# All exponent biases on VectorE in a fused attention and mixing kernel, with the order, bank and engine tables set anew

## The chip, the cores and the metric

The kernel runs on one core of one Trainium2 chip. The metric is the device time of one execution in microseconds. A core has TensorE (PE in the profile, with its weight loads as PEld), VectorE (DVE), ScalarE (ACT), GpSimd (POOL) and SyncE (SP), which here issues all DMAs. The engines run their own instruction lists in order and wait for each other by semaphores.

## What is computed

Attention over 8 batches of 8 heads with 576 positions of 64 channels, with a mask by blocks of 64 positions; then, for each batch, a mixing layer on the 576x512 result x:

```python
scores = scale * np.matmul(q, k.transpose(0, 1, 3, 2))
scores = np.where(block_i >= block_j, scores, -1000000000.0)
attn = np.exp(scores - np.max(scores, axis=-1, keepdims=True))
attn = attn / (np.sum(attn, axis=-1, keepdims=True) + 1e-09)
x = np.matmul(attn, v)                       # heads side by side: (B, 576, 512)
theta = x @ w_theta
y = w_tok_r @ (x * cos(theta)) + w_tok_i @ (x * sin(theta))
u = x + y
out = u + np.maximum(u @ w_ch, 0.0)
```

## The kernel before

**Parts.** The work is cut into some 3,400 parts, each of which issues one to some tens of instructions. Three tables of literals decide everything about them that is not fixed by the mathematics: `ORDER` is the sequence in which the parts are issued (each engine gets its instructions in this sequence), `BANKS` says which PSUM bank each result takes, and `PLACES` gives, for each part that has a choice, the engine: A is ScalarE, P is GpSimd, D is VectorE. `emit` reads the tables and calls the parts. Nothing is decided on the chip.

**A head of attention.** Heads come in pairs p, head n = 2p and 2p + 1. TensorE makes the scores (line 589, with the mask at 596 and the first block at 617) in PSUM (`s` and `g` are banks). VectorE takes the maxima of the four or five row tiles (`m`, line 633). The bias of the exponential, -scale times the maximum plus a constant, is one small instruction on `m` of 128 x 2 to 128 x 5 elements (line 641), part `mn`; ScalarE then makes the exponentials `t` (line 646), which wait for it. A copy in 16 bits `p` (the part `high`, line 431 on ScalarE, 433 elsewhere) and the rest of the difference (`low`, line 436) follow, SyncE issues a transposing DMA (`pt<-p`), and TensorE multiplies with v (`weighted`, line 680). VectorE divides by the sum (lines 692, 694 and 698) into `xn`. The first 16 heads have two pieces, A and B, with a bias each; the other 48 have one: 80 biases in all. The first three batches (24 heads) use a constant scale, the later ones a scale from the tile `size`.

**The mixing of a batch.** `xn` is split (`xp`, lines 431, 433 and 436), transposed by DMA (`xT`), and TensorE makes theta (816, 819). ScalarE and VectorE make the turns (828, 834), their absolute values (440 on ScalarE, 442 on VectorE) and the sines (849, 851). `z`, the product with x (line 860, GpSimd or VectorE), is split into `zh` and `zl`; TensorE mixes tokens (884), `u` is collected on VectorE (893, after `x_again`, line 889, on GpSimd or VectorE), split (423 or 427, and 900), and multiplied with the channel weights (907); the result goes out by 913 or 915 and 923. Once at the start, the weights are unpacked and split (lines 471 to 507).

The bias and its reader, and the line that adds the part with its choice of engines:

```python
        def bias(self, piece, on):                                          # line 638
            engine_of(on).tensor_scalar(out=self.m[:, NI + a:NI + b], in0=self.m[:, a:b],
                scalar1=self.scales()[1], scalar2=math.log(LIFT), op0=ALU.mult, op1=ALU.add)
...
            nc.scalar.activation(out=t_parts[self.hh][:, to:to + n], in_=self.scores_of(i), func=AF.Exp,
                scale=self.scales()[0], bias=self.m[:, NI + i:NI + i + 1])   # line 646
...
                add(("mn", n, piece), step_of(h.bias, piece), known + [("m", n, i) for i in mine], on="DP")
```

Of the kernel before, what the change touches and what calls it, by code (L numbers as in the profile page):

```python
# [37 lines left out]
    8, 160, 158, 16, 9, 10, 11, 17, 18, 335, 363, 339, 364, 372, 373, 374, 340, 0, 1, 350, 351, 19, 12, 352, 353,  # L38
    375, 336, 387, 2, 334, 361, 3, 362, 365, 24, 337, 386, 32, 33, 25, 56, 338, 341, 392, 376, 342, 26, 57, 40, 58,
    41, 366, 367, 20, 27, 162, 42, 4, 343, 368, 5, 48, 59, 49, 28, 391, 390, 354, 50, 43, 163, 13, 344, 21, 29, 34,  # L40
    385, 51, 35, 369, 415, 164, 401, 60, 165, 414, 388, 345, 72, 413, 44, 104, 64, 136, 88, 96, 80, 161, 346, 347,
    105, 106, 402, 403, 412, 166, 416, 167, 168, 389, 36, 65, 73, 89, 97, 423, 169, 52, 74, 170, 171, 172, 159, 90,
    393, 66, 394, 98, 332, 81, 355, 82, 137, 107, 75, 348, 437, 395, 67, 37, 396, 397, 398, 138, 120, 424, 333, 99,
    112, 383, 45, 53, 349, 404, 377, 76, 83, 384, 139, 100, 356, 61, 14, 91, 417, 84, 418, 68, 92, 69, 357, 441, 77,
    358, 85, 425, 359, 93, 101, 465, 370, 141, 151, 466, 121, 122, 436, 113, 176, 142, 143, 178, 144, 94, 371, 114,
    115, 439, 419, 360, 78, 378, 420, 489, 440, 116, 22, 399, 438, 443, 62, 123, 6, 38, 494, 379, 464, 421, 442,
    444, 380, 173, 452, 447, 445, 434, 540, 463, 467, 446, 145, 15, 128, 140, 426, 427, 174, 381, 468, 469, 70, 405,
    406, 474, 152, 453, 108, 448, 30, 487, 31, 435, 470, 449, 454, 86, 455, 456, 180, 400, 124, 129, 130, 471, 491,
    490, 495, 407, 514, 408, 409, 410, 488, 382, 475, 428, 476, 477, 478, 545, 496, 1804, 492, 422, 450, 497, 493,
# [12 lines left out]
    650, 673, 631, 604, 669, 611, 693, 1854, 1869, 651, 670, 646, 1855, 645, 656, 657, 1864, 639, 612, 613, 698,
    614, 1857, 1865, 652, 678, 658, 632, 564, 691, 1862, 196, 1858, 1859, 692, 633, 586, 615, 1863, 626, 653, 679,
    680, 681, 694, 695, 689, 659, 699, 700, 660, 682, 654, 661, 696, 701, 1908, 697, 1909, 744, 634, 1866, 721, 674,
    702, 1910, 720, 197, 1899, 729, 1914, 1915, 730, 707, 718, 635, 1870, 191, 1867, 1916, 1900, 1873, 1901, 199,
    636, 1871, 683, 690, 703, 719, 708, 709, 1885, 637, 675, 710, 722, 200, 676, 2004, 2007, 1881, 201, 119, 655,
    662, 663, 664, 665, 711, 1911, 749, 1884, 704, 1912, 705, 712, 1880, 2005, 155, 1907, 731, 1877, 1902, 723, 684,
    1893, 1917, 724, 202, 1903, 1894, 1895, 725, 1888, 1872, 1896, 1897, 1918, 1892, 666, 1898, 1913, 677, 203,
    1904, 2008, 1889, 2006, 1882, 685, 1919, 743, 1890, 1876, 1878, 1886, 1879, 742, 686, 1874, 1875, 1905, 687,
    726, 727, 785, 195, 732, 747, 748, 745, 746, 750, 753, 204, 706, 713, 205, 1944, 765, 714, 715, 716, 754, 751,  # L70
    752, 755, 733, 1945, 756, 764, 767, 766, 157, 1938, 1887, 1883, 1939, 734, 1940, 206, 768, 688, 771, 1946, 2009,
    790, 757, 1941, 758, 772, 769, 1891, 770, 773, 193, 1947, 207, 135, 208, 1937, 192, 1948, 1949, 1942, 1943, 717,
    2010, 735, 728, 736, 737, 738, 740, 739, 741, 783, 784, 786, 826, 2023, 788, 787, 789, 791, 2024, 759, 808,
# [24 lines left out]
    2123, 2124, 2125, 244, 2126, 968, 982, 2265, 969, 1041, 2143, 2150, 2127, 2151, 2128, 985, 970, 2135, 2257,
# [1078 lines left out]
```

## Time and profile before

| what | value |
|---|---|
| time, median of 3 runs (least to most) | 674.0 us (673.57 to 674.95) |
| time of the profiled execution | 677.03 us |
| its span, first to last instruction | 675.2 us |
| TensorE busy | 614.8 us, 91% |
| VectorE busy | 586.5 us, 87% |
| ScalarE busy | 508.3 us, 75% |
| GpSimd busy | 374.3 us, 55% |
| mean granted clock of TensorE | 0.964 |

The profiled execution is 3.0 us longer than the median, and its span is 1.8 us shorter than its own time. Busy shares are averages; the program has a start in which weights and inputs arrive, a long middle in which the heads of one batch run beside the mixing of the batch before, and an end that only mixes the last batch.

### The profile page before, as it was taken

How to read it: one execution, taken by the hardware profiler on the slowest of the kernel's cores; microseconds unless marked ns; L12 is line 12 of the kernel's file. 1: busy time of each engine (PE TensorE's matmuls, PEld its weight loads, DVE VectorE, ACT ScalarE, POOL GpSimd, SP SyncE). 2: the span in 40 equal slices, each digit the busy share in tenths (PEclk: the TensorE clock that was granted, in tenths of full speed). 3: DMA queues.
4: the chain of work that ended last, by engine and by line, in shares of the span. 5: the costliest groups of instructions: out<-in, count | busy, mean ns of one | idle time of the engine just before them, and what ended most of it. 6: DMA issues, size and time to landing. Idle time of an engine off the chain costs nothing.

```text
span 675.2 us, 18061 instructions
## 1 busy us (share of the span) xinstructions
PE 614.8 (91%) x7374; PEld 456.1 (68%) x7374; DVE 586.5 (87%) x1162; ACT 508.3 (75%) x770; POOL 374.3 (55%) x391
## 2 busy tenths in 40 slices
PE   5376688998999999999999998999899999999997
PEld 3155545785688577775787756785677477867775
DVE  3988889998997999989998899999998999976554
ACT  5888669885987998877998799979987997225021
POOL 2463536853667467961677628744593457931530
PEclk9577788999999999999999999999999999999999
DMA  8999999899969688879789977999779547930003
GB/s 349 336 264 224 196 196 225 183 202 187 202 141 237 132 190 188 183 157 185 202 178 154 206 168 169 199 165 213 169 177 184 93 81 161 189 78 2 19 1 123
DMA packets 268515, 116.58 MB, mean 173 GB/s; under 512 B 256016, under 2 KB 256016, under 8 KB 268432
## 3 DMA queue, kind: packets, MB, share of 16 engines
q1 hardware_dynamic: 268432, 115.43, 79.1%
q8 instruction: 57, 0.93, 0.6%
q14 instruction: 26, 0.21, 0.1%
HBM read 42.01 MB, written 9.44 MB: 76 GB/s over the span
## 4 chain that ended last, share of the span: by engine, by line
PE 52%; DVE 22%; DMA 10%; ACT 8%; POOL 4%; issue 4%; SPq 1%; ACTq 0%; POOLq 0%; DVEq 0%
PE g L884 12%; PE s L884 8%; DMA pt<-p 7%; PE g L680 7%; DVE m L633 5%; PE g L816 5%; PE g L907 5%; PE s L589 4%; PE s L907 4%; DVE p L436 3%; PE s L816 3%; ACT t L646 3%; PE g L589 2%; DMA xT<-xp 2%; PE s L819 1%
## 5 line engine op out<-in xcount | busy, mean ns | idle before, releaser
L884 PEld LDWEIGHTS <-zh 128*128 128x128 f16 x1152 | 112.7, 98 | 29.8 <-issue 1.1
L884 PE MATMUL g<-wT_h,zh 128*128 128x288 f16 x405 | 115.9, 286 | 1.0 <-DVE u L893 0.8
L884 PE MATMUL g<-wT_h,zl 128*128 128x288 f16 x405 | 115.8, 286 | 0.1
L884 PE MATMUL g<-wT_l,zh 128*128 128x288 f16 x405 | 115.8, 286 | 0.0
L680 PE MATMUL g<-v,pt 128*128 128x65 f16 x2880 | 102.9, 197 | 13.3 <-DMA pt<-p 6.5
L680 PEld LDWEIGHTS <-pt 128*128 128x128 f16 x2880 | 99.0, 100 | 20.3 <-DMA pt<-p 10.3
L633 DVE TENSOR_REDUCE m<-s 128x1 f32<-128x576 f32 (+2 forms) x132 | 85.3, 672 | 6.9 <-PE s L596 6.9
L436 POOL TENSOR_TENSOR p<-t,p 128x512 f16<-128x512 f32 (+4 forms) x28 | 66.5, 2376 | 43.8 <-ACT p L431 38.9
L431 ACT CAST p<-t 128x1600 f16<-128x1600 f32 (+4 forms) x66 | 84.3, 1283 | 8.5 <-DMA pt<-p 4.4
L436 DVE TENSOR_TENSOR p<-t,p 128x1600 f16<-128x1600 f32 (+4 forms) x52 | 84.9, 1635 | 5.0 <-ACT p L431 3.5
L860 POOL TENSOR_TENSOR aa<-aa,xn 128x256 f32<-128x256 f32 (+1 forms) x59 | 48.3, 832 | 60.3 <-ACT aa L849 44.4
L816 PEld LDWEIGHTS <-xT 128*128 128x128 f16 x384 | 36.6, 99 | 46.9 <-DMA xT<-xp 4.3
L884 PEld LDWEIGHTS <-zl 128*128 128x128 f16 x576 | 56.3, 98 | 16.3 <-issue 1.6
L646 ACT ACTIVATE t<-s,m,size 128x576 f32<-128x576 f32 (+1 forms) x80 | 59.1, 778 | 7.8 <-POOL m L641 6.5
L907 PEld LDWEIGHTS <-wch_h 128*128 128x128 f16 x512 | 48.1, 98 | 15.8 <-issue 2.8
L633 DVE TENSOR_REDUCE m<-g 128x1 f32<-128x192 f32 (+2 forms) x156 | 54.4, 372 | 4.5 <-PE g L596 4.4
L646 ACT ACTIVATE t<-g,m,size 128x320 f32<-128x320 f32 (+2 forms) x100 | 49.0, 535 | 11.9 <-DVE m L641 5.7
L436 POOL TENSOR_TENSOR zl<-aa,zh 128x512 f16<-128x512 f32 (+1 forms) x36 | 40.8, 1139 | 15.3 <-ACT zh L431 9.5
L884 PE MATMUL s<-wT_h,zh 128*128 128x288 f16 x171 | 48.9, 286 | 0.0
L884 PE MATMUL s<-wT_l,zh 128*128 128x288 f16 x171 | 48.9, 286 | 0.0
L884 PE MATMUL s<-wT_h,zl 128*128 128x288 f16 x171 | 48.9, 286 | 0.0
L907 PE MATMUL g<-uh,wch_h 128*128 128x288 f16 x160 | 45.8, 286 | 1.4 <-DVE u L893 0.8
(194 smaller groups left out, 1624.3 us busy)
## 6 DMA issues: line engine op xcount, KB each, us to landing
rv<-in_v SPq DMA_DIRECT2D x16, 768.0 KB, 5.4
rq<-in_q SPq DMA_DIRECT2D x16, 640.0 KB, 5.1
rk<-in_k SPq DMA_DIRECT2D x16, 576.0 KB, 5.0
out<-xT SPq DMA_DIRECT2D x32, 288.0 KB, 2.8
w_raw<-in_w_tok SPq DMA_DIRECT2D x5, 576.0 KB, 6.7
pt<-in_w_tok SPq DMA_DIRECT2D x4, 576.0 KB, 8.5
w_raw<-in_w_theta SPq DMA_DIRECT2D x4, 512.0 KB, 7.0
w_raw<-in_w_ch SPq DMA_DIRECT2D x4, 512.0 KB, 4.7
```

What stands on the lines that cost most here:

```text
L431: nc.scalar.copy(out=out, in_=x)
L436: engine_of(on).tensor_tensor(out=out, in0=x, in1=y, op=ALU.subtract)
L589: nc.tensor.matmul(to[hh][:, col:col + n], lhsT=qq[rows, P + P * i:P + P * i + P], rhs=kk[rows, k0:k0 + n], start=nn == 0 and col % 512 == ...
L633: nc.vector.tensor_reduce(out=self.m[:, i:i + 1], in_=self.scores_of(i), axis=AX.X, op=ALU.max)
L646: nc.scalar.activation(out=t_parts[self.hh][:, to:to + n], in_=self.scores_of(i), func=AF.Exp, scale=self.scales()[0], bias=self.m[:, NI + ...
L680: nc.tensor.matmul(o[:, i, :], lhsT=source[:, block, :], rhs=vv[:, slot, hh, :], start=first, stop=last)
L816: nc.tensor.matmul(g, lhsT=xT[:, xx + i, :], rhs=ww[:, dt, :], start=first, stop=last)
L819: nc.tensor.matmul(g[half * D:half * D + D, 0:HC], lhsT=xT[:, xx + i, 0:D], rhs=ww[:, dt, half * HC:half * HC + HC], start=first, stop=last)
L860: engine_of(on).tensor_tensor(out=cd, in0=cd, in1=self.xns[dt][:, i0:i0 + ni, :], op=ALU.mult)
L884: nc.tensor.matmul(g, lhsT=zz[:, kk, cols], rhs=ww[:, kk, ts], start=(n == 0 and kk == k0 and nn == 0), stop=n == 4 and kk == k0 + ni - 1 ...
L907: nc.tensor.matmul(g[:, 0:HS], lhsT=ww[:, dt, e * P:(e + 1) * P], rhs=uu[:, dt, th * HS:(th + 1) * HS], start=dt == 0 and n == 0, stop=dt ...
```

## The change

The code of the parts is the same. All three tables have other numbers, so that the order on every engine, the banks and the engines of other parts differ too. Of the 80 biases, 33 were on VectorE and 47 on GpSimd; now all 80 are on VectorE. The parts with a choice, before and after (A ScalarE, P GpSimd, D VectorE), as the tables give them:

| part | before | after |
|---|---|---|
| `mn`, bias | P 47, D 33 | D 80 |
| `high` | A 66, P 10, D 4 | A 65, P 8, D 7 |
| `low` | P 28, D 52 | P 23, D 57 |
| `z` | P 103, D 57 | P 111, D 49 |
| `zh` | A 43, P 26, D 11 | A 53, P 21, D 6 |
| `zl` | P 57, D 23 | P 58, D 22 |
| `x_again` | P 15, D 17 | P 19, D 13 |
| `xp`, both halves | A 21, P 26, D 17 | A 20, P 23, D 21 |
| absolute values of turns | A 28, D 12 | A 24, D 16 |
| first half of v | A 24, P 4, D 4 | A 16, P 13, D 3 |
| first half of u | A 20, P 8, D 4 | A 18, P 9, D 5 |
| first halves of q and k | A 25, P 11, D 4 | A 31, P 7, D 2 |
| unpacking and scaling of weights | A 24, P 12, D 15 | A 31, P 14, D 6 |

```diff
 ORDER = [
-    8, 160, 158, 16, 9, 10, 11, 17, 18, 335, 363, 339, 364, 372, 373, 374, 340, 0, 1, 350, 351, 19, 12, 352, 353,
...
 PLACES = (
-    "DAAPDAADPDDPAAAADDDADADAAAPDAPPDAPDPPAAPADAAPAAPADAADAPPADPPDPDPAPPPDAPPADDPDADADDPPDADPPPAPADDPDPAPPAPAPDDDAPPA"
...
+    "ADAAAAADPPAPAADPAAPAAPAAPAAADAADPAAAPAAADPPAPAAPAAPADDDDPDDPPDPDPDADDADDADDDDPDADDAPDAPDDPDDADDAPDAPDAPADADDAPDA"
```

**Heads 30 and 31 on VectorE**, some 280 us after the start, before the change (`p_99` and `p_100` are the `low` of an even and an odd head, here 30 and 29; the biases of both heads are on GpSimd here):

```order
L436 TENSOR_TENSOR p_100<-t_98,p_100 128x1536
L692 TENSOR_SCALAR r<-g_114 128x5
L633 TENSOR_REDUCE m<-s_110 128x1
L694 RECIPROCAL r<-r 128x5
L726 TENSOR_REDUCE size<-size 128x3
L633 TENSOR_REDUCE m<-g_112 128x1
L893 SCALAR_TENSOR_TENSOR u_3974<-g_111,size_tok,u_3974 128x288
L633 TENSOR_REDUCE m<-g_112 128x1
L382 TENSOR_REDUCE size<-g_111 128x3
L384 TENSOR_SCALAR size<-size 128x3
L387 TENSOR_SCALAR size<-size 128x3
L436 TENSOR_TENSOR p_99<-t_97,p_99 128x1600
```

The same place after the change:

```order
L633 TENSOR_REDUCE m<-s_110 128x1
L860 TENSOR_TENSOR aa<-aa,xn 128x2x128
L743 SCALAR_TENSOR_TENSOR size<-size,size_theta 128x1
L633 TENSOR_REDUCE m<-s_110 128x1
L641 TENSOR_SCALAR m<-m,size 128x4
L726 TENSOR_REDUCE size<-size 128x3
L893 SCALAR_TENSOR_TENSOR u_3943<-g_113,size_tok,u_3943 128x288
L692 TENSOR_SCALAR r<-g_114 128x5
L694 RECIPROCAL r<-r 128x5
L698 TENSOR_TENSOR xn<-g_114,r 128x5x64
L382 TENSOR_REDUCE size<-g_111 128x3
L436 TENSOR_TENSOR p_99<-t_97,p_99 128x1600
```

The bias of head 31 now stands on VectorE right behind the last of its maxima and ahead of the `low` of head 30 (`p_99`).

**The last two heads on VectorE** (62 and 63), some 574 us after the start, before:

```order
L923 SCALAR_TENSOR_TENSOR xT<-u_8605,size,s_109 128x288
L436 TENSOR_TENSOR p_99<-t_97,p_99 128x1600
L915 TENSOR_SCALAR g_113<-g_113,size 128x288
L923 SCALAR_TENSOR_TENSOR xT<-u_8110,size,g_113 128x288
L573 SCALAR_TENSOR_TENSOR v_88<-rv,size,v_87 128x12x64
L692 TENSOR_SCALAR r<-g_114 128x5
L694 RECIPROCAL r<-r 128x5
L698 TENSOR_TENSOR xn<-g_114,r 128x5x64
L860 TENSOR_TENSOR aa<-aa,xn 128x128
L915 TENSOR_SCALAR g_111<-g_111,size 128x288
L889 TENSOR_TENSOR u_9364<-xT 128x576
L692 TENSOR_SCALAR r<-g_114 128x5
```

After:

```order
L573 SCALAR_TENSOR_TENSOR v_86<-rv,size,v_85 128x12x64
L923 SCALAR_TENSOR_TENSOR xT<-u_8106,size,g_111 128x288
L860 TENSOR_TENSOR aa<-aa,xn 128x128
L436 TENSOR_TENSOR p_99<-t_97,p_99 128x1600
L436 TENSOR_TENSOR zl<-aa,zh 128x512
L692 TENSOR_SCALAR r<-g_114 128x5
L860 TENSOR_TENSOR rr<-rr,xn 128x2x128
L694 RECIPROCAL r<-r 128x5
L698 TENSOR_TENSOR xn<-g_114,r 128x5x64
L436 TENSOR_TENSOR p_100<-t_98,p_100 128x1536
L436 TENSOR_TENSOR zl<-rr,zh 128x512
```

Before, only head 62 has its `low` on VectorE (the row `p_99`), followed by an `x_again` (L889); now head 63 has its `low` there too (`p_100`), and the `x_again` is elsewhere.

**VectorE at the start**, some 20 to 30 us after it, among the unpacking of weights (L481, L485, L501) and the first maxima, before:

```order
L481 TENSOR_SCALAR w_raw<-w_raw 128x576
L485 SCALAR_TENSOR_TENSOR w_val<-w_val,pt_107 128x576
L485 SCALAR_TENSOR_TENSOR w_val<-w_val,w_raw 128x576
L485 SCALAR_TENSOR_TENSOR w_val<-w_val,pt_106 128x576
L436 TENSOR_TENSOR p_100<-t_98,p_100 128x1024
L633 TENSOR_REDUCE m<-g_113 128x1
L641 TENSOR_SCALAR m<-m 128x2
L501 TENSOR_SCALAR wT_h<-w_val 128x576
L633 TENSOR_REDUCE m<-g_113 128x1
L633 TENSOR_REDUCE m<-s_109 128x1
L633 TENSOR_REDUCE m<-s_110 128x1
```

After:

```order
L633 TENSOR_REDUCE m<-g_111 128x1
L633 TENSOR_REDUCE m<-g_114 128x1
L485 SCALAR_TENSOR_TENSOR w_val<-w_val,pt_106 128x576
L633 TENSOR_REDUCE m<-g_112 128x1
L633 TENSOR_REDUCE m<-s_110 128x1
L641 TENSOR_SCALAR m<-m 128x2
L501 TENSOR_SCALAR wth_h<-w_val 128x512 x2
L633 TENSOR_REDUCE m<-g_112 128x1
L485 SCALAR_TENSOR_TENSOR w_val<-w_val,pt_107 128x576
L633 TENSOR_REDUCE m<-g_111 128x1
L485 SCALAR_TENSOR_TENSOR w_val<-w_val,w_raw 128x576 x2
L641 TENSOR_SCALAR m<-m 128x2
```

One bias (L641) stood among these rows; now there are two, and two more between the rows ahead of these, in place of biases on GpSimd.

## Rows read from the trace of the kernel before

**Rows 1.** The page: busy us, share of the span, instructions per engine.

```profile
PE 614.8 (91%) x7374; PEld 456.1 (68%) x7374; DVE 586.5 (87%) x1162; ACT 508.3 (75%) x770; POOL 374.3 (55%) x391
```

**Rows 2.** Windows: length, busy us (instructions) per engine, granted clock, DMA share, GB/s.

```profile
0.00:125.00 125.00, 84.40 (x913) 58.58 (x914) 103.77 (x223) 96.98 (x159) 59.02 (x90) 0.81 1.01 249
125.00:575.00 450.00, 434.21 (x5584) 323.59 (x5581) 418.01 (x825) 386.30 (x575) 276.01 (x267) 1.00 0.85 175
575.00:675.20 100.20, 96.20 (x888) 73.88 (x884) 64.73 (x116) 25.06 (x38) 39.22 (x37) 0.99 0.28 67
...
400.00:425.00 25.00, 22.41 (x358) 17.15 (x354) 24.35 (x49) 23.74 (x33) 19.06 (x21) 1.00 0.72 151
525.00:550.00 25.00, 22.98 (x240) 14.54 (x238) 24.74 (x45) 24.57 (x37) 14.03 (x13) 1.00 0.50 92
```

**Rows 3.** The page: chain that ended last, share of the span by engine.

```profile
PE 52%; DVE 22%; DMA 10%; ACT 8%; POOL 4%; issue 4%; SPq 1%; ACTq 0%; POOLq 0%; DVEq 0%
```

**Rows 4.** Line 641, the biases: count, ns least/median/most, first and last start.

```profile
L641 POOL TENSOR_SCALAR m<-m x25: 191/294/1116, 11.1 to 203.7; 128x2 f32<-128x2 f32 x18, 128x3 f32<-128x3 f32 x3, 128x5 f32<-128x5 f32 x3, 128x4 f32<-128x4 f32 x1
L641 POOL TENSOR_SCALAR m<-m,size x22: 269/275/1929, 248.7 to 571.5; 128x4 f32<-128x4 f32 x11, 128x5 f32<-128x5 f32 x11
L641 DVE TENSOR_SCALAR m<-m,size x18: 192/302/1226, 224.3 to 557.5; 128x5 f32<-128x5 f32 x9, 128x4 f32<-128x4 f32 x9
L641 DVE TENSOR_SCALAR m<-m x15: 151/169/1941, 18.3 to 182.9; 128x2 f32<-128x2 f32 x6, 128x3 f32<-128x3 f32 x5, 128x4 f32<-128x4 f32 x3, 128x5 f32<-128x5 f32 x1
```

**Rows 5.** Waits: who waited for whom, total us, times, longest.

```profile
ACT t L646 <- POOL m L641: 16.9, 19, 3.0
ACT t L646 <- DVE m L641: 16.2, 12, 4.7
...
DVE u L893 <- PE g L884: 10.7, 8, 3.5
PEld L680 <- DMA pt<-p: 10.3, 10, 2.4
...
DVE u L893 <- PE s L884: 10.1, 8, 2.7
```

**Rows 6.** Timeline of VectorE and GpSimd at 26, 556 and 160 us.

```profile
26.57 1.94 DVE L641 TENSOR_SCALAR m<-m 128x2 f32<-128x2 f32 x1
...
26.20 2.28 POOL L436 TENSOR_TENSOR p<-t,p 128x1088 f16<-128x1088 f32 x1 [6.48 <-ACT p L431]
...
557.53 1.23 DVE L641 TENSOR_SCALAR m<-m,size 128x4 f32<-128x4 f32 x1
...
555.62 3.10 POOL L436 TENSOR_TENSOR p<-t,p 128x1536 f16<-128x1536 f32 x1
...
160.92 0.17 DVE L641 TENSOR_SCALAR m<-m 128x5 f32<-128x5 f32 x1
```

**Rows 7.** VectorE's groups: busy us, mean ns of one, idle before.

```profile
L641 DVE TENSOR_SCALAR m<-m,size 128x5 f32<-128x5 f32 x9 | 4.0, 441 | 0.2
...
L889 DVE TENSOR_TENSOR u<-xT 128x576 f32<-128x576 f16 x17 | 18.3, 1075 | 0.1
...
L860 DVE TENSOR_TENSOR aa<-aa,xn 128x256 f32<-128x256 f32 x29 | 14.5, 505 | 0.0
...
L436 DVE TENSOR_TENSOR p<-t,p 128x1600 f16<-128x1600 f32 (+4 forms) x52 | 84.9, 1635 | 5.0 <-ACT p L431 3.5
```

**Rows 8.** Timeline at 281 to 289 us: GpSimd, VectorE, ScalarE.

```profile
284.07 1.93 POOL L641 TENSOR_SCALAR m<-m,size 128x4 f32<-128x4 f32 x1
...
284.12 1.83 DVE L436 TENSOR_TENSOR p<-t,p 128x1600 f16<-128x1600 f32 x1
...
286.03 1.02 ACT L646 ACTIVATE t<-g,m,size 128x320 f32<-128x320 f32 x2 [2.14 <-POOL m L641]
```

**Rows 9.** Chain in time: start us, us, what; first and last GpSimd bias.

```profile
32.18 0.19 POOL m L641
...
524.30 0.28 POOL m L641
```

More of the change, by code (lines that the diff above doesn't have):

```diff
@@ L37 @@
 ORDER = [
[176 rows of a table removed]
[176 rows of a table added]
 ]
 BANKS = (
-    "5064556406401235601234601235401235601234501230101236401236501234601236501235601235401235601235401236501236501234"
-    "6012356012345012364012356012346012364012345012365012354012364012356012356012354012365012345256416041444565640601"
-    "5460114565666400654160425114445344454666166240165566554506655104502141064066556041425110660526466456611400541625"
-    "63463210534066451601352025430645142"
+    "6640455415101234601234501235401235401236501230101236401235601234601236501236401236501234601234501235401234501234"
@@ L220 @@
+    "5012356012354012364012346012346012345012356012356012364012356012364012346012354012365012356246515041550565440441"
+    "5460560214666650466150524616666244541656064530665500455604466101503640144155446541520126505646466544456100451342"
+    "31315450463621054620463501434154206"
 )
 PLACES = (
-    "DAAPDAADPDDPAAAADDDADADAAAPDAPPDAPDPPAAPADAAPAAPADAADAPPADPPDPDPAPPPDAPPADDPDADADDPPDADPPPAPADDPDPAPPAPAPDDDAPPA"
-    "DPAPADAPPAPPADPPDDDADPADPADPAPPDADPAPPADPAPPPADDADPDAPDPPDPADDADAPADPAPADADADDAPAAADADPAPDAAPADPADPPAPADPADAPADA"
@@ L224 @@
-    "DPADAPADDDDAPAAADADDAPPDDPADDADAPADAPDADAPAPADPADAAADADPPDPAAPADPADAAAPADPADAPAPADPADAAPPADDAPPAADADDADAAAPDDDAP"
-    "AAADADPAPAADPADDPPPDAPADPAPADAPADAPAADAAPPPPPPAPPPAPDPADDDAPDDAPPDAPDDAPDPADPPAPDADPPPDAAAADDAAAADAPAPDDAAAAADPP"
-    "PDPPPDDAPDPAPDPPPDDPPDDAPPPADPPADPDADDADAPAPDADADADAAAPAPAPDDAAADADDPPPPAPPDPPPPDPPPAPPPAPDPAPDPAPPPPDPPDPDPDAPP"
-    "PPAAAAADAAPPAPADDDDADAAPPPPDDPPDDPPDDPDPPAPPPAPPPAPPPAPPPAPPPADPAPADPDADAADDAADADPPPPPPAADADPPAPPDPPPPAPPPPDPPPP"
-    "DPAPPDAPPDADPDPDPPAPPADAPPDADAADADADAPADAPPPAADDAPPPDDPAPPPPPDPADDPPPDDAPPPAPDPAPPPDPPPAPPAPDPADAAADDADDAPPADAPA"
@@ L229 @@
-    "DAAADAPPADDPPPPDPPPPDPPPPPDDDPPPPDDDPDPDPPDDADDAPDDADDDAAADDADPPADAPDDDAADDDDDDPDPPDDDDPPDPPDDDPPAPPPADPPDDPPADP"
-    "PDPPADADPPADADAADAD"
+    "ADAAAAADPPAPAADPAAPAAPAAPAAADAADPAAAPAAADPPAPAAPAAPADDDDPDDPPDPDPDADDADDADDDDPDADDAPDAPDDPDDADDAPDAPDAPADADDAPDA"
+    "DDPDADAPDAPDADDPDDDADDADDADDAPADADDADDADDAPADADDADPDADDDDPDADDADADADDADAADDADDAPAAPDADDAPAAADADDADPPADADDADAPADA"
+    "PDADAAADDDDAPAAADADDAPPDPDADDADAAADAPDADADPDPDDADAAPDADDPDPAADADDADAAPDADDADAAPDADDPDAAPDADDAPAAADADDADAAADADDDP"
@@ new lines @@
+    "AAADDDDAPAAPDAPDAPPPPDADDADDDAPADAPADDAAPDDDPPAPPPAPPDADPPDPDDAPDPADDDAPPPADPPAPPADPPDDAAAAAADADADADAPDPAAAAAPDP"
+    "PPDAPPPAPPPAPPPDDDPAPDDPDDPAPPPADPPPPPADAPAPAADDDAADAPDADAPDDDAAAAPPAPDPAPDPADDDAPPPPPDDAPPPADDPAPPDAPPPPPPPPAPP"
+    "PDDAAAADAAPPPDAPDDADADDPPAPPDAPPDPPDPAPPPAPPDAPPPAPDDPPPPADPDAPPAPPDPDADAAADDADAPAPAPAPAADDDPPADPPPPPPAPDPAPPPAP"
+    "DPAPPPAPDPAPPDADPPAPPPDADPPADDDDADADAPADAPAPAADDDPDPPPPAPPPPPDPAPPPPPPPAPDDADPPAPPPAPDPAPDADPDDPAAAADAAAAPDADDPA"
+    "DAAADAPPADPDADPPADPDADPDPPPPPDPDPPPDDPPPPPPPPPPAPADAPDADDAADADPDDPPPADDDADADPPDDDDPPPAPPPPDDPPPPPPDPPPPDDDPPDAPP"
@@ L231 @@
+    "PADPDDAPADPDADDAAAA"
 )
```

351 rows, old and new, of the table ORDER are left out of this document.

## The prediction

> **What bounds the kernel now.** I read the page's busy line first, then the same by stage, then the chain, and last the rows of the line that is changed. TensorE is busy for 91% of the span and VectorE for 87% [rows 1]. By stage [rows 2] these are three different programs. In the first 125 us TensorE works 84.4 us, at a granted clock of 0.81 on the average, with the DMA share at 1.01 and VectorE at 103.8 us: the inputs and VectorE's unpacking of them are the limit. From 125 to 575 us TensorE is busy for 434.2 of 450 us and VectorE for 418.0, so that both are nearly full, TensorE 15.8 us short and VectorE 32.0. In single stretches VectorE is the fuller one: 24.35 against 22.41 of 25 us at 400, 24.74 against 22.98 at 525. After 575 us TensorE is full (96.2 of 100.2) and VectorE is not (64.7): here the last batch is mixed, and its amount of TensorE work is fixed. The end therefore moves by what TensorE is kept idle before some 590 us, and by nearly nothing else. The chain that ended last lies on TensorE for 52%, on VectorE for 22% and on GpSimd for 4% of the span [rows 3]; 22% of 675.2 is 148.5 us, a quarter (0.25) of VectorE's 586.5 busy us.
>
> **What is removed.** GpSimd loses 47 biases, 25 with a median of 0.29 us and 22 with one of 0.28, and the longest took 1.93 [rows 4]. GpSimd is 55% busy, so its time is worth little; what counts is who waited. ScalarE waited 16.9 us for these biases in 19 waits, and 16.2 us in 12 waits for those on VectorE [rows 5]: per wait the VectorE ones are not shorter, so the hop between engines is not what costs. On the chain, GpSimd's biases are eight pieces, 3.8 us together, the first 0.19 us and the last 0.28 [rows 9]; half of it is one piece at 284 us: the bias of head 31 begins at 284.07, VectorE's `low` of head 30 at 284.12, and both end within 0.1 us of each other, 1.9 us later; ScalarE stood 2.14 us before its exponentials [rows 8]. In the new order that bias stands ahead of this `low` on VectorE itself, so this wait goes. Eight pieces on VectorE at its median of some 0.24 us (between 0.169 and 0.302 [rows 4]) would be 1.9 us: the chain gains 3.8 - 1.9 = 1.9 us. For the ends: nothing, if the bias is now late for other reasons, and 3.8 if it is always hidden.
>
> **What is added.** VectorE gets 47 biases. At its medians, 25 x 0.169 + 22 x 0.302 = 10.9 us. The low bound is the bias that nothing disturbs, 0.16 us (0.17 at 160.92 [rows 6]; the least are 0.151 and 0.192 [rows 4]): 47 x 0.16 = 7.5. The high bound is the mean of the group that was disturbed most evenly, 0.441 [rows 7]: 20.7. The difference is a GpSimd instruction that was under way: the bias at 26.57 took 1.94 us and ended at 28.51, GpSimd's `low` beside it at 28.48; that at 557.53 took 1.23 and ended at 558.76, the `low` at 558.72 [rows 6]. I take the medians, since most of the 33 were short. Whatever is queued behind such a bias on VectorE, the next maxima, `u` and `low`, waits with it.
>
> The trace agrees there with the Trainium skill (SBUF — State Buffer, section "Who interferes with whom"): VectorE in a two-port mode, which `tensor_scalar` can enter, and GpSimd hold a shared pair of ports by turns, and the one that comes second is blocked for the whole instruction. That rule speaks against this change: it moves a small instruction that has to wait its turn from an engine that is 55% busy to one that is 87% busy. By it, the sum below would be made with the high bound instead of the medians; this is the third rival.
>
> The other pieces on VectorE nearly cancel. Five more `low` at 1.635 us are +8.2, eight fewer `z` at 0.505 are -4.0, four fewer `x_again` at 1.075 are -4.3 [rows 7]. Of the small ones, fourteen go (weights 9, `zh` 5) and eleven come (values of turns 4, `xp` 4, `high` 3); at the size of a `z` that is -1.5. Together -1.6. ScalarE and GpSimd take over what goes; ScalarE ends with about as much as before (ten more `zh`, eight fewer v), and both have room outside the middle.
>
> TensorE's list has the same instructions in nearly the same order, and the loads come in nearly the same order too, so nothing is booked for them. At the start more biases stand between VectorE's unpacking of weights and its maxima; they are in the 47. At the end, `low` of head 63 is now VectorE's, where GpSimd's took some 3 us in the like case (3.10 [rows 6]) against 1.83 on VectorE [rows 8]: a gain of 1.3 us for the last head, which I count at nothing, since TensorE has the rest of batch 6 to do meanwhile and is full there [rows 2].
>
> **The sum.** VectorE: 10.9 - 1.6 = +9.3 us (from 5.9 to 19.1). How much of it reaches the end? At today's share of the chain, a quarter: 2.3 us. All of it, if VectorE becomes the limit of the middle: 9.3. VectorE's idle 32.0 us there contain 20.8 us of waiting for TensorE's mixing before `u` [rows 5], which shrink when VectorE is late; but TensorE has only 15.8 us idle, in the stretches in which VectorE is at 24.4 and 24.7 of 25 already. I take one half, 4.6 us, between a quarter and all. Less the 1.9 us of the chain this is +2.7 us. The profiled execution would then take 677.0 + 2.7 = 679.7, and the median, which is 3.0 us lower, 674.0 + 2.7 = 676.7 us. With a quarter on the path it is 674.4, with all of 9.3 it is 681.4.
>
> **The rivals.** First, faster: the new tables take out waits beyond the bias itself. If all 3.8 us of GpSimd's biases on the chain are hidden, if ScalarE's 16.9 us of waits for them go and count by ScalarE's 8% of the chain (1.4 us), and if TensorE gets back a third of its 10.3 us of waits for transposed tiles (3.4 us), with VectorE's additional work put into its own 20.8 us of waits, the time is 674.0 - 8.6 = 665.4; with half of that, 669.7. For it speaks that the order was set anew around the new place, as at head 31; against it that VectorE had least room just where TensorE idles. It decides as soon as less than a fifth of the 9.3 us reaches TensorE. Second, no difference: a quarter of 9.3 us against the 1.9 us gained, 674.4 us, 673.5 with a little less. The order of the other parts would then only follow the biases. Third, clearly slower: each moved bias meets a GpSimd instruction and holds up VectorE for 0.44 us; 20.7 - 1.6 = 19.1 us, of which half or more arrive: 674.0 + 9.6 - 1.9 = 681.7, and 691 with all of it. Against it speaks that most of VectorE's biases so far were short. That the change does not do what it says is excluded by the order: GpSimd's list has no bias left.
>
> **Chances.** Slower by some 1.4 to 7 us, as forecast, 0.36; clearly slower, 0.14; no difference that can be measured, 0.18; faster, 0.32. A measurement of this kernel can tell some 0.2% (1.3 us) from no change. So faster 0.32, same 0.18, slower 0.50. The likeliest case alone reaches from 675.4 to 681; the range of 668 to 687 takes in half of the first rival's gain and some more, and the third up to between its half and its whole, and leaves out less than 2 in 10.
>
> **What would show it.** Right: VectorE's busy time at about 596 us (592 to 606), GpSimd's near 350, VectorE's share between 125 and 575 us at 94 to 96%, TensorE's idle time in that stage up by 2 to 4 us, and line 641 on VectorE x80 with a median of 0.2 to 0.3 us and some of over a microsecond ending with a GpSimd instruction. ScalarE's waits for line 641 would be all on VectorE and hardly less than 33 us together. Wrong: TensorE's idle time in the middle falls below 15 us, or the first 125 us hold clearly more TensorE work than 84 us; then the gain came from the order and not from the bias. If VectorE's busy time is far over 600 us, the third rival holds.

## The result, and the profile after

The changed kernel takes 682.8 us (median of 4 runs, 681.66 to 685.62) against 674.3 us for the kernel before (4 runs, 673.57 to 674.95): a ratio of 1.0126, 95% interval 1.0106 to 1.0146. It is slower by 8.5 us, where 2.7 were forecast. The profiled execution took 681.66 us with a span of 679.8, that of before 677.03 with 675.2: the two profiles lie only 4.6 us apart, and the first stages must be read with that in mind (below).

The page's busy line of after, to be held against [rows 1]:

```profile
PE 612.6 (90%) x7372; PEld 452.9 (67%) x7374; DVE 600.6 (88%) x1196; ACT 508.5 (75%) x777; POOL 343.2 (50%) x350
```

VectorE has gained 14.1 us and GpSimd lost 31.1. The windows of after, with the columns of [rows 2], for the three stages and the stretch of 550 to 575 us:

```profile
0.00:125.00 125.00, 83.73 (x928) 56.19 (x931) 112.12 (x245) 99.80 (x165) 55.44 (x74) 0.86 1.01 253
125.00:575.00 450.00, 428.06 (x5516) 319.22 (x5516) 424.82 (x840) 379.21 (x567) 245.23 (x229) 1.00 0.82 173
575.00:680.00 105.00, 100.77 (x931) 77.45 (x928) 63.66 (x114) 29.50 (x47) 42.55 (x48) 1.00 0.28 68
...
550.00:575.00 25.00, 18.90 (x234) 14.34 (x233) 22.69 (x38) 13.47 (x21) 15.87 (x12) 0.93 0.62 116
```

The same stretch of the kernel before:

```profile
550.00:575.00 25.00, 25.00 (x363) 19.75 (x357) 23.97 (x47) 20.19 (x31) 15.59 (x14) 1.00 0.68 134
```

In the middle stage TensorE's idle time went from 15.8 to 21.9 us. The 6.1 us of difference are those 25 us alone: TensorE was full there before and is 6.1 us short now. In the rest of the stage, taken together, VectorE's additional work made TensorE no idler. What stands in the hole is told by the chain of after, in order of time (start us, us, what):

```profile
551.06 2.79 DVE size L746
556.39 5.14 PE g L884 x27
...
564.19 2.67 DVE rr L860
567.97 1.87 DVE m L633 x4
569.87 2.32 DVE m L641
```

Three instructions of VectorE: the size of a chain of scales (128 x 1), a `z`, and the bias of head 62. The timeline of after beside them, GpSimd, VectorE, ScalarE and TensorE:

```profile
550.74 3.10 POOL L436 TENSOR_TENSOR p<-t,p 128x1536 f16<-128x1536 f32 x1 [6.00 <-issue]
...
550.98 2.88 DVE L746 TENSOR_TENSOR size<-size,u_scales 128x1 f32<-128x1 f32 x1
...
555.32 1.31 ACT L646 ACTIVATE t<-g,m,size 128x320 f32<-128x320 f32 x3 [4.04 <-DVE r L692]
...
556.39 0.28 PE L884 MATMUL g<-wT_h,zh 128*128 128x288 f16 x1 [3.12 <-ACT t L646]
...
557.26 0.45 PE L884 MATMUL g<-wT_h,zl 128*128 128x288 f16 x1
...
562.87 3.71 POOL L436 TENSOR_TENSOR p<-t,p 128x1600 f16<-128x1600 f32 x1 [5.90 <-ACT p L431]
...
564.10 2.76 DVE L860 TENSOR_TENSOR rr<-rr,xn 128x256 f32<-128x256 f32 x1
...
569.07 3.10 POOL L436 TENSOR_TENSOR p<-t,p 128x1536 f16<-128x1536 f32 x1 [2.49 <-issue]
...
569.87 2.32 DVE L641 TENSOR_SCALAR m<-m,size 128x5 f32<-128x5 f32 x1
...
568.03 0.31 PE L589 MATMUL g<-kh,qh 64*128 64x320 f16 x2 [1.47 <-DVE xT L923]
572.66 0.28 PE L907 MATMUL g<-uh,wch_h 128*128 128x288 f16 x1 [1.52 <-DVE xT L923]
```

GpSimd's `low` (line 436; the expectations below call it the cast low) of heads 59, 60 and 61 begins first each time, the VectorE instruction second, and the second ends with the first or just behind it: 550.74 + 3.10 = 553.84 and 550.98 + 2.88 = 553.86; 566.58 and 566.86; 572.17 and 572.19. An instruction of one element in a partition was held for 2.88 us, where the same one took 0.14 in the kernel before. Behind it wait a maximum, the bias of head 60, the exponentials (ScalarE 4.04 us idle) and TensorE's mixing (3.12 us). The two other gaps of TensorE, 1.47 and 1.52 us, end with an instruction of VectorE (line 923) that stands behind the held `z` and behind the held bias in its queue; the three make up the 6.1 us. In this execution TensorE also paid at a lower clock: shortly after those 3.12 us of idling its matmuls go from 0.28 to 0.45 us, and the granted clock from 557 to 561 us is 0.57, so most of it is the lower of the two levels, 1.2 GHz. That did not come back: in the second profile of the same kernel (e8 below) TensorE idles for the same 3.12 us, and the clock behind it stays at 1.00. First after's window, then the gap and the window of e8:

```profile
557.00:561.00 4.00, 4.00 (x22) 2.62 (x20) 3.13 (x7) 3.09 (x6) 0.00 (x0) 0.57 0.90 173
```

```profile
561.03 0.28 PE L884 MATMUL g<-wT_h,zh 128*128 128x288 f16 x1 [3.12 <-ACT t L646]
...
562.00:566.00 4.00, 4.00 (x49) 3.30 (x47) 3.89 (x9) 3.07 (x6) 0.00 (x0) 1.00 0.98 188
```

The biases themselves, line 641 of after, and who waited for them, to be held against [rows 4, 5]:

```profile
L641 DVE TENSOR_SCALAR m<-m x40: 151/169/1137, 12.3 to 202.9; 128x2 f32<-128x2 f32 x24, 128x3 f32<-128x3 f32 x8, 128x5 f32<-128x5 f32 x4, 128x4 f32<-128x4 f32 x4
L641 DVE TENSOR_SCALAR m<-m,size x40: 189/232/2324, 224.2 to 574.5; 128x5 f32<-128x5 f32 x20, 128x4 f32<-128x4 f32 x20
...
ACT t L646 <- DVE m L641: 32.1, 24, 4.7
```

Head by head (start of TensorE's product with v, line 680, after less before) the loss of this profile has one place. After is 2.8 us ahead at head 8 (its larger piece begins at 97.30, the product of before at 100.11). The profile of before has a wait of its own there for a transposed tile, which those of after, e7 and e8 show with 0.46 us, 0.42 us or not at all. The row of before:

```profile
92.64 0.60 PE L816 MATMUL g<-wth_h,xT 128*128 128x512 f16 x2 [2.36 <-DMA xT<-xp]
```

It is 3.4 ahead at head 57 (546.85 against 550.23 us) and 6.0 behind at head 62 (593.20 against 587.21). Of this one execution the whole loss, 9.4 us, lies between head 57 and head 62: 6.1 us of it is the idling, and the lower clock an estimated 1.6 (14 matmuls at steps of 0.24 us instead of 0.12). A second profile of after (e8) lost 3.2 us from head 8 to 57 and 6.3 from there to 62.

### The profile page after: what moved, and what is told of

Its sections match the earlier page's. It is cut to its first block, busy times and chain, and to the rows that moved or that the text cites. A ratio compares the mean times of both kernels' runs of the same rounds, so it can differ in the third digit from the quotient of the medians.

```text
span 679.8 us, 18059 instructions
## 1 busy us (share of the span) xinstructions
PE 612.6 (90%) x7372; PEld 452.9 (67%) x7374; DVE 600.6 (88%) x1196; ACT 508.5 (75%) x777; POOL 343.2 (50%) x350
## 5 line engine op out<-in xcount | busy, mean ns | idle before, releaser
L680 PE MATMUL g<-v,pt 128*128 128x65 f16 x2880 | 101.1, 195 | 13.7 <-DVE xn L698 8.3
L884 PE MATMUL g<-wT_h,zh 128*128 128x288 f16 x369 | 106.5, 289 | 5.7 <-ACT t L646 3.8
L884 PE MATMUL g<-wT_h,zl 128*128 128x288 f16 x369 | 106.5, 289 | 0.0
L884 PE MATMUL g<-wT_l,zh 128*128 128x288 f16 x369 | 106.5, 289 | 0.0
L436 POOL TENSOR_TENSOR p<-t,p 128x512 f16<-128x512 f32 (+4 forms) x23 | 54.3, 2368 | 68.7 <-ACT p L431 40.8
L431 ACT CAST p<-t 128x1536 f16<-128x1536 f32 (+4 forms) x65 | 82.2, 1273 | 2.8 <-DMA pt<-p 1.7
L884 PE MATMUL s<-wT_h,zh 128*128 128x288 f16 x207 | 59.3, 287 | 1.9 <-ACT t L646 1.9
L884 PE MATMUL s<-wT_l,zh 128*128 128x288 f16 x207 | 59.3, 287 | 0.0
L884 PE MATMUL s<-wT_h,zl 128*128 128x288 f16 x207 | 59.3, 286 | 0.0
L907 PEld LDWEIGHTS <-wch_h 128*128 128x128 f16 x512 | 48.3, 98 | 16.2 <-issue 3.9
L633 DVE TENSOR_REDUCE m<-g 128x1 f32<-128x320 f32 (+2 forms) x156 | 54.3, 371 | 4.4 <-PE g L596 4.3
L907 PE MATMUL g<-uh,wch_l 128*128 128x288 f16 x172 | 49.3, 286 | 0.0
```

The lines of the kernel that those rows point to most:

```text
L431: nc.scalar.copy(out=out, in_=x)
L436: engine_of(on).tensor_tensor(out=out, in0=x, in1=y, op=ALU.subtract)
L633: nc.vector.tensor_reduce(out=self.m[:, i:i + 1], in_=self.scores_of(i), axis=AX.X, op=ALU.max)
L680: nc.tensor.matmul(o[:, i, :], lhsT=source[:, block, :], rhs=vv[:, slot, hh, :], start=first, stop=last)
L884: nc.tensor.matmul(g, lhsT=zz[:, kk, cols], rhs=ww[:, kk, ts], start=(n == 0 and kk == k0 and nn == 0), stop=n == 4 and kk == k0 + ni - 1 ...
L907: nc.tensor.matmul(g[:, 0:HS], lhsT=ww[:, dt, e * P:(e + 1) * P], rhs=uu[:, dt, th * HS:(th + 1) * HS], start=dt == 0 and n == 0, stop=dt ...
```

## The experiments

All ratios are to the kernel before on the same chip. The letters of the theories are those of the expectations. First the change was taken apart: the new place without the new order (e1), the new order without the new place (e2).

**e1: the order and banks of before, the 47 biases on VectorE.** Each of the 47 letters goes from P to D, as in the last row with such a letter:

```diff
-    "AAADADPAPAADPADDPPPDAPADPAPADAPADAPAADAAPPPPPPAPPPAPDPADDDAPDDAPPDAPDDAPDPADPPAPDADPPPDAAAADDAAAADAPAPDDAAAAADPP"
+    "AAADADDAPAADDADDPPPDADADDAPADAPADAPAADAAPPPPPPAPPPAPDPADDDAPDDAPPDAPDDAPDPADPPAPDADPPPDAAAADDAAAADAPAPDDAAAAADPP"
```

> The order and the banks of the kernel before, with one edit: the 47 biases that stood on GpSimd are on VectorE, at the same places of the order; all other engines are as before. Theory A, the biases themselves cost (VectorE's load, and its waiting for GpSimd instructions under way): slower than before by 4 to 10 us (ratio 1.006 to 1.015), VectorE's busy time up by 11 to 20 us. Theory B, the loss came from the other moves of the new tables: within 2 us of before (ratio 0.997 to 1.003), the busy time up all the same.

Measured: 695.6 us, ratio 1.0287 (1.0257 to 1.0317). The place alone costs 20 us. Both expected ranges missed. Most of the loss comes in steps: against before, TensorE's product falls back by 3.7 us at heads 13 and 14, 3.7 at head 48, 1.7 at 51, 4.1 at 58 and 3.1 at 60 and 61; from head 14 to 47 it loses 3.1 us in smaller ones. e7 below, which adds the load alone, shows none of those from head 51 on.

**e2: after, with the same 47 back on GpSimd** (the letters D to P in the tables of after).

> The order and the banks of the changed kernel, with one edit: the same 47 biases are back on GpSimd; all other engines are as after the change. Theory A: faster than the changed kernel by 4 to 10 us, so 673 to 679 us. Theory B: no faster than the changed kernel, 681 us or more, since the order was made for biases on VectorE and GpSimd's long instructions now stand ahead of some of them.

Measured: 693.6 us, ratio 1.0273 (1.0242 to 1.0305), by the ratios some 8 to 10 us slower than after, as theory B expected. GpSimd now stands still for maxima in 24 waits, with its other work behind; before it was 28.0 us in 14 waits:

```profile
POOL m L641 <- DVE m L633: 59.5, 24, 8.9
```

So the new tables are fitted to the new place and the old to the old. They had won back some 10 of e1's 20 us.

**e3: after, with the `low` of heads 59, 60 and 61 on VectorE** (three letters, P to D).

> The changed kernel with one edit: the differences (line 436, p) of heads 59, 60 and 61, which stand on GpSimd between 550 and 572 us of its trace, are on VectorE. In that trace three VectorE instructions end with them: 2.79 us for a 128x1 product, 2.67 us for a z, 2.32 us for the bias of head 62. Theory B (long GpSimd instructions at the end hold VectorE up, whatever it does): faster than the changed kernel by 3 to 7 us, 676 to 680 us, and TensorE busy for over 23 of 25 us from 550 to 575. Theory A (VectorE's load): no gain, 682 us or more, for VectorE has 3 x 1.8 us more to do.

Measured: 681.6 us, ratio 1.0084 (1.0058 to 1.0111), between the two expected ranges and by the ratios some 3 to 4 us faster than after. The holds are gone (0.14, 0.41 and 0.23 us), but VectorE carries the three `low` instead, and TensorE is busy for only 20.00 of the 25 us at 550, where theory B expected over 23 and after has 18.90.

**e4: before, with the 47 biases on ScalarE.**

```diff
+            if on == "A": nc.scalar.activation(out=self.m[:, NI + a:NI + b], in_=self.m[:, a:b],
+                func=AF.Identity, scale=self.scales()[1], bias=lift)
```

> The order and the banks of the kernel before, with one edit: the 47 biases that stood on GpSimd are on ScalarE (an activation with Identity, the scale and a constant tile), which is idle some of the time and reads them itself. Theory A in the form of ports (a small instruction on VectorE costs because it has to wait for GpSimd's): ScalarE's biases do not wait for GpSimd, 672 to 676 us. Theory A in the form of plain load (any engine that is nearly full in the middle loses by 47 more instructions): 676 to 680 us. Theory B: within 2 us of before.

Measured: 689.0 us, ratio 1.0203 (1.0174 to 1.0233), above all three expected ranges, although none of these biases is stretched:

```profile
L641 ACT ACTIVATE m<-m,lift x25: 279/296/313, 11.5 to 210.5; 128x2 f32<-128x2 f32 x18, 128x3 f32<-128x3 f32 x3, 128x5 f32<-128x5 f32 x3, 128x4 f32<-128x4 f32 x1
L641 ACT ACTIVATE m<-m,lift,size x22: 375/391/402, 256.0 to 580.2; 128x4 f32<-128x4 f32 x11, 128x5 f32<-128x5 f32 x11
```

By the ratio that is 13.7 us slower than before. Either ScalarE's own load or GpSimd's earlier start (below) may be the cause; no run here parts them.

**e5 and e6: queue place.** In e1 the waits from the last maximum's end to the bias's start sum to 69.7 us, since other instructions stand between. In e5 (before) and e6 (after) all 80 biases are on VectorE, directly behind their last maxima. One of the moves in e5, where 1503 is the bias of head 50 and 1482 the `low` of head 49:

```diff
-    ... 1580, 1535, 1501, 1520, 1517, 1482, 1503, 1518, ...
+    ... 1580, 1535, 1501, 1503, 1520, 1517, 1482, 1518, ...
```

> The kernel before with all 80 biases on VectorE, each standing in the order directly behind the last maxima that it needs, nothing else changed. Theory Q (a bias costs what it waits in VectorE's queue behind longer instructions: the same 80 biases at the places of before took 20 us more, and their sum from the maxima's end to the bias's start was 69.7 us): that sum falls below 25 us, and the time comes to 674 to 680 us, against 695.6 with the biases at the old places. Theory L (a bias costs VectorE's time and its stretching beside GpSimd, wherever it stands): 47 more instructions remain on VectorE, its busy time stays near 606 us, and the time is 685 us or more.

> The kernel after with all 80 biases directly behind the last maxima that each needs, nothing else changed. Theory Q: the sum of the waits from maxima to bias falls from 75 us below 25, and the kernel is faster than after by 4 to 10 us (673 to 679 us). Theory L: nothing of the load or of the stretching has changed, within 2 us of after (681 to 685 us); the hole at 550 to 575 us stays in either, since its three held instructions are still beside GpSimd's casts.

Measured: e5 694.1 us, 1.0293 (1.0268 to 1.0317); e6 683.6 us, 1.0135 (1.0105 to 1.0164). The sums fell to 2.8 and 3.5 us, and the times did not move. As the account of the 20 us, theory Q falls. At one place it held: e1's step of 3.7 us at head 48 is 0.3 in e5, where the move shown above takes the bias of head 50 ahead of the `low` of head 49 (more under e9). What was won there went elsewhere. The steps of e5 at heads 58, 59 and 61 (4.0, 1.7, 1.6 us) are nearly those of e1, and a new one of 2.6 us at head 36 has this beside it, on GpSimd and VectorE:

```profile
359.11 3.10 POOL L436 TENSOR_TENSOR p<-t,p 128x1536 f16<-128x1536 f32 x1
...
359.11 3.12 DVE L641 TENSOR_SCALAR m<-m,size 128x5 f32<-128x5 f32 x1
```

**e7: the load alone.** Before, complete, and VectorE makes the 47 a second time, into a tile that nobody reads.

```diff
             engine_of(on).tensor_scalar(out=self.m[:, NI + a:NI + b], ...)
+            if on == "P": nc.vector.tensor_scalar(out=spare[:, a:b], ...)
```

> The kernel before, complete, with 47 further instructions on VectorE: the bias of each maximum that GpSimd makes is made a second time on VectorE, at the same place of the order, into a tile that nobody reads. No exponential waits for them, so what they cost is VectorE's time and stretching alone. Theory L: 47 at 0.23 us are 10.9 us and with the stretching more, and the time rises by 5 to 12 us (679 to 687 us). Theory Q: by 0 to 3 us (674 to 678 us), since the 20 us of the biases at these places were the exponentials' waiting.

Measured: 680.5 us, ratio 1.0082 (1.0061 to 1.0102), in theory L's range. The load costs 5.5 us in the old order, so it is not nothing, and it is not the 20 us either. e7 has no step at heads 58 to 61.

**e8: after again**, beside e5 to e7, unchanged.

> The kernel after, unchanged, beside the three others on one chip: both theories expect 681 to 685 us, 1.010 to 1.015 of before. It gives the base for the second of these runs, and a second profile of the hole at 550 to 575 us: if the three held VectorE instructions there belong to the order, they are there again with 2 to 3 us each.

Measured: 684.4 us, ratio 1.0149 (1.0125 to 1.0174). The hole is there again, with TensorE busy for 19.59 of the 25 us from 550, but with two of the three holds: the size takes 2.87 us and the bias of head 62 2.27. The `z` (567.07, 0.41 us) comes ahead of GpSimd's `low` (567.50) this time and is not held. So two holds are enough for a hole of 5.4 us, and whether the `z` is held changes from one execution to the next.

**e9: which of the two is read.** The instructions of e7, but the exponentials read VectorE's result, and GpSimd's 47 are the spare ones.

```diff
-            engine_of(on).tensor_scalar(out=self.m[:, NI + a:NI + b], ...)
+            if on == "P": nc.gpsimd.tensor_scalar(out=spare[:, a:b], ...)
+            nc.vector.tensor_scalar(out=self.m[:, NI + a:NI + b], ...)
```

> The kernel before, complete: all 80 biases read by the exponentials are made on VectorE, and GpSimd still makes its 47 as well, at the same places of the order, into a tile that nobody reads. Each engine's instructions are those of the run with 47 spare biases on VectorE (680.5 us, 1.0082); only which of the two results the exponentials wait for is changed. Theory H (the 14 us more of the run with all biases on VectorE come from GpSimd: without its own bias, which stood ahead and waited for the same maxima, it begins its next long instruction, a cast of low, at once, and the bias on VectorE is held until that one ends, as at 567.56 us for 2.58 us): GpSimd stays in step, no bias is held by a cast that it did not meet before, and the time is 677 to 684 us, 1.005 to 1.012. Theory W (the exponentials wait longer for a bias that VectorE makes, whatever GpSimd does): 688 to 696 us.

Measured: 684.3 us, ratio 1.0127 (1.0105 to 1.0150). Putting 47 useless instructions back on GpSimd makes e1 faster by 11 us (1.0287 to 1.0127). Head 60 in three kernels shows how. Before, GpSimd and ScalarE: GpSimd makes the bias and only then starts its `low` at 555.62 [rows 6].

```profile
555.27 0.27 POOL L641 TENSOR_SCALAR m<-m,size 128x5 f32<-128x5 f32 x1 [6.40 <-DVE m L633]
...
555.58 1.02 ACT L646 ACTIVATE t<-g,m,size 128x320 f32<-128x320 f32 x2 [1.03 <-POOL m L641]
```

e1, GpSimd, VectorE, ScalarE (the 567.56 us of the expectation is 566.50 in the trace): with no bias ahead, the `low` starts while VectorE still takes the last maxima, and the bias is held until it ends (569.05 and 569.08).

```profile
565.96 3.09 POOL L436 TENSOR_TENSOR p<-t,p 128x1536 f16<-128x1536 f32 x1 [6.76 <-issue]
...
566.50 2.58 DVE L641 TENSOR_SCALAR m<-m,size 128x5 f32<-128x5 f32 x1
...
569.18 1.02 ACT L646 ACTIVATE t<-g,m,size 128x320 f32<-128x320 f32 x2 [3.35 <-DVE m L641]
```

e9: the spare bias waits for the maxima, keeps the `low` back, and VectorE's bias is through in 0.23 us (line 642 there).

```profile
560.57 0.23 DVE L642 TENSOR_SCALAR m<-m,size 128x5 f32<-128x5 f32 x1
...
560.71 0.28 POOL L641 TENSOR_SCALAR spare<-m,size 128x5 f32<-128x5 f32 x1 [6.61 <-DVE m L633]
561.06 3.12 POOL L436 TENSOR_TENSOR p<-t,p 128x1536 f16<-128x1536 f32 x1
...
560.90 1.02 ACT L646 ACTIVATE t<-g,m,size 128x320 f32<-128x320 f32 x2 [0.99 <-DVE m L642]
```

Theory H holds for 11 of e1's 20 us. e9 came out just above what H expected, and 3 us above e7, with intervals that do not overlap. The profiles show one place for it: at head 48, e9 falls back by 4.4 us against before and e7 by 0.8. There, where the exponentials of head 50 are due just ahead of that product, the order has the `low` of head 49 ahead of the bias of head 50 on VectorE, so that GpSimd's spare bias begins at 460.80 and VectorE's, which is read, only at 463.50. VectorE, GpSimd, ScalarE and TensorE of e9:

```profile
461.55 2.02 DVE L436 TENSOR_TENSOR p<-t,p 128x1536 f16<-128x1536 f32 x1
463.50 0.72 DVE L642 TENSOR_SCALAR m<-m,size 128x5 f32<-128x5 f32 x1
...
460.80 0.27 POOL L641 TENSOR_SCALAR spare<-m,size 128x5 f32<-128x5 f32 x1 [0.65 <-DVE m L633]
...
464.25 1.45 ACT L646 ACTIVATE t<-s,m,size 128x576 f32<-128x576 f32 x2 [3.67 <-DVE m L642]
...
465.75 0.70 PE L816 MATMUL s<-wth_h,xT 128*128 128x512 f16 x2 [2.90 <-ACT t L646]
```

That is theory Q's queue place, at this one head. The granted clock from 466.2 to 469.4 us, right behind this gap, is 0.50. In e7, where GpSimd's bias is read, ScalarE waits 0.42 us for it at this place. The 20 us of e1 are then some 5.5 of load, 3 of queue place and 11 of GpSimd's earlier start; the 3 rest on one profile each of e7 and e9, and on the same step in e1 and its absence in e5.

**e10: the hole filled.** After, with GpSimd's three `low` held back: each is preceded by a copy of one element a partition that VectorE has just written.

```diff
...
+            if self.n in HELD: nc.gpsimd.tensor_copy(out=spare, in_=HELD[self.n]())
             less(on, lo, x, hi)
```

> The kernel after, complete, with three of GpSimd's instructions held back: ahead of the cast low of heads 59, 60 and 61 it copies one element a partition that VectorE writes (the bias of head 60, the reciprocal of head 58, the bias of head 62), so that each cast begins behind the VectorE instruction which it held in the profile of after (2.88, 2.76 and 2.32 us instead of about 0.14, 0.4 and 0.2). Nothing is moved on VectorE, ScalarE or TensorE. Theory H: the hole at 550 to 575 us goes, TensorE's 6 us of idle time there with it, and the time falls by 3 to 6 us from after, 678 to 681 us, 1.005 to 1.010. Theory of load alone: VectorE is full there with or without the holding, within 1.5 us of after (1.011 to 1.016). If the casts, now late, are waited for themselves (heads 59 to 61 in TensorE's turn), it is slower than after.

Measured: 678.3 us (12 runs, 676.48 to 680.61), ratio 1.0044 (1.0027 to 1.0060). Between 5.5 and 7 us of after's loss (8.5 us at 1.0126, 10 at 1.0149) go with three added instructions. The size and the bias are short again, and TensorE has 23.26 us. VectorE, GpSimd, ScalarE of e10 (its added lines move the numbers: 748 is before's 746, 642 is 641, 647 is 646), and its window:

```profile
555.67 0.15 DVE L748 TENSOR_TENSOR size<-size,u_scales 128x1 f32<-128x1 f32 x1
...
556.39 0.23 DVE L642 TENSOR_SCALAR m<-m,size 128x5 f32<-128x5 f32 x1
...
556.68 0.19 POOL L662 COPY spare<-m 128x1 f32<-128x1 f32 x1 [7.25 <-DVE r L694]
556.83 3.11 POOL L436 TENSOR_TENSOR p<-t,p 128x1536 f16<-128x1536 f32 x1
...
556.72 1.32 ACT L647 ACTIVATE t<-g,m,size 128x320 f32<-128x320 f32 x3 [0.74 <-DVE r L694]
```

```profile
550.00:575.00 25.00, 23.26 (x346) 18.23 (x346) 23.78 (x50) 19.86 (x31) 16.44 (x14) 1.00 0.61 108
```

**e11: six held back.** After, with e10's three and three more, each of which held a bias in the profile of after, for 1.21, 1.14 and 0.83 us. The edit is one table of pairs, the held instruction's part and the part that it waits for:

```diff
+HELD = {1707: 1728, 1735: 1694, 1752: 1773, 2122: 918, 529: 554, 1892: 707}
```

> The kernel after, complete, with six of GpSimd's instructions held back by the same copy of one element: the three casts as before (678.3 us, 1.0044), and three that held a bias for 1.21, 1.14 and 0.83 us (the sums of group x, tile 1, behind the bias of head 24; the cast low of head 7's second part behind the bias of head 8; the sums of tile 0 behind the bias of head 14). Theory H: TensorE idles 1.3 us behind the first in the profile of after, and the other two lie where TensorE waits for heads 5 to 12 anyway, so it gains 0.5 to 2 us more: 676 to 678 us, 1.001 to 1.004. If the held-back ones are waited for themselves, it is 679 us or more.

Measured: 677.6 us, ratio 1.0029 (1.0014 to 1.0045), as expected in size, though its interval and e10's overlap.

**e12: the same remedy on the kernel before**, at two places.

```diff
+HELD = {347: 401, 2879: 329}
```

> The kernel before, complete, with two of GpSimd's instructions held back in that way: the cast low of head 0 behind the bias of head 2 on VectorE (held 1.94 us there, and TensorE waited 5.8 us right behind), and a two-input step of tile 5 behind the scale of tile 7 (held 1.16 us, TensorE's gap 0.91). Theory H: up to 0.9 us at the second place, and between 0 and 1.5 at the first, where other waits are near: 672.5 to 675 us, 0.997 to 1.000. If holding back costs more than the lock, 676 us or more.

Measured: 674.3 us (12 runs, 671.36 to 675.76) against 675.3 (23 runs), ratio 0.9976 (0.9960 to 0.9993): the fastest kernel of this study, by a margin at the edge of what can be told. At the second place, head 55 comes 1.0 us earlier, of which 0.5 are lost again at head 56: the scale of batch 7 (the expectation says tile) took 1.16 us in before (521.06) and takes 0.15 in e12 (line 740 of before, 746 there; VectorE, then GpSimd).

```profile
519.30 0.15 DVE L746 SCALAR_TENSOR_TENSOR size<-size 128x1 f32<-128x1 f32 x1
...
519.51 0.19 POOL L328 COPY spare<-size 128x1 f32<-128x1 f32 x1 [0.19 <-DVE size L746]
```

At the first place the bias is short too (0.15 us), but heads 1 to 3 come 1.5 to 3.0 us later and head 7 on time: nothing gained that the traces show. So the traces show some 0.5 us of the remedy, where the medians are 1.0 apart.

## Why the prediction was right in sign and short in size

**The bound** was read rightly: VectorE and TensorE nearly full in the middle, the end set by TensorE's idle time before some 590 us. After 575 us TensorE is full again (100.77 of the 104.8 us that are left).

**The removed part**: GpSimd's busy time came to 343.2 us (350 forecast). ScalarE's waits for line 641 are 32.1 us, as they were 16.9 + 16.2. The wait at head 31 went as foreseen: its bias takes 0.23 us in after. The 1.9 us gained on the chain can't be seen by themselves.

**The added part**: the medians came at 0.169 and 0.232 us, near the 0.169 and 0.302 that were booked, but the sum was not made of medians. The 80 biases take 28.3 us, the 33 of before 12.4: 15.9 us more where 10.9 were booked, a mean of 0.34 between the low bound 0.16 and the high one 0.44. The other pieces came as -1.8 (-1.6 booked), VectorE's busy time as 600.6 (596 forecast, 592 to 606).

**The step that failed** is the sum's "one half" of VectorE's additional time on the path, 4.6 us. It treats the load and the holding as one quantity, spread evenly. The runs part them. What is left without the hole is small: after stands at 1.0044 then, and at 1.0029 with six held back, 3.0 and 2.0 us over before, near the +2.7 that were forecast for everything. The holding is not spread: three GpSimd instructions in one stretch of 25 us cost 5.5 to 7 us, not far from the time for which they held VectorE in the profile of after (7.2 us beyond what the three held instructions take undisturbed), because maxima, bias, exponentials and mixing stand behind. Two of the three held are no biases at all. The high bound multiplied 47 biases by a mean and so could not contain them; [rows 6] showed the mechanism, 1.94 and 1.23 us on a bias, and the prediction asked how many biases would meet it, not which other instruction would when GpSimd's timing shifts. So the sign came out by another path than the one that was summed: most of the loss is this stretch and not the spread load. That the sum with all of the 9.3 us, 681.4, lies near the 682.8 measured is luck.

**The third rival** came nearest (681.7), by its mechanism, though not as it put it: not each bias meets a GpSimd instruction, most take 0.17 to 0.23 us. Its point of decision is the order, which of the two comes first. That is what the rule of the Trainium skill says (SBUF — State Buffer, section "Who interferes with whom"): issue order decides who blocks. The traces agree where VectorE began clearly later: it ended with GpSimd, 2.88 us for 0.14. Where the two starts lie close together they don't tell: at 284 us it was GpSimd's bias that took 1.93 us, though its recorded start is 0.05 us ahead of VectorE's [rows 8].

**The first rival** (faster) asked for less than a fifth of the load on the path. In the profile of after the load did nearly vanish from head 8 to 57, but the second profile of after and e10 lose 3.2 and 1.8 us there.

**What would show it**: VectorE's share in the middle is 94.4% (94 to 96 forecast); TensorE's idle time there rose by 6.1 us, not 2 to 4, all of it in one stretch; the first 125 us hold 83.73 us of TensorE's work (84.4 before), as forecast.

Open: the cause of e4's loss, why the same idle time cost clock in one profile of after and not in the other, and what the last 2 to 3 us of e10 and e11 are.

## What to carry to other kernels

An instruction that leaves a queue lets what stood behind it start earlier, perhaps just ahead of something that it then holds. Where VectorE and GpSimd work side by side, look in the trace for short VectorE instructions that end together with a long one of GpSimd, and ask for each which engine waits behind it. If the long one is not urgent, a copy of one element can hold it back until the short one is through; three such copies gave back 5.5 of 8.5 us here, or 7 of 10 by the second measurement of after. And an instruction that others wait for belongs ahead of a long one in its own queue: a bias behind a `low` cost some 4 us at one head (e9).

## What was not expected of the hardware

That size hardly matters to the one that is held: 128 x 1 and 128 x 256 elements on VectorE took 2.88 and 2.76 us, each behind one instruction of GpSimd, and ended 0.02 and 0.28 us behind it. That a bias on ScalarE beside the same GpSimd work is never stretched (0.279 to 0.402 us in e4). And that the same idle time of TensorE can cost clock or not: 3.12 us of it were followed by a stretch (557 to 561 us) at a granted clock of 0.57 in after and at 1.00 in e8, and 2.90 us in e9 by one at 0.50.
